# Turning normalised rows by transposing DMA transfers instead of PE products in an attention and GLU kernel

## The chip, the cores and the metric

The kernel runs on one core of one Trainium2 chip. The metric is the device time of one execution in microseconds (us): lower is better. The time given for a kernel is the median of several executions. The kernel before took 911.5 us, the median of three (910.59, 911.5 and 912.72).

The core has a matrix engine (PE; its weight loads are listed apart as PEld), a vector engine (DVE), a scalar engine (ACT), a general engine (POOL), and SP, which here only issues DMA transfers. Each engine runs its own list of instructions in order; one engine waits for another on semaphores.

## The reference

One transformer block on 2048 rows of 640 columns (bf16), with 32 heads of 20 columns each:

```
ln(x) = (x - mean) / sqrt(var + 1e-5)          # over the 640 columns
q, k, v = split(ln(x) @ wqkv)                  # 640 x 1920
p = softmax(q @ k.T * 20**-0.5)                # per head, 2048 x 2048
h = x + concat_heads(p @ v) @ wo
out = h + ((ln(h) @ w_gate) * (ln(h) @ w_up)) @ w_down      # 1728 hidden columns
```

So there are two normalisations. "Layer 1" below is the attention half, "layer 2" the gated half. In each the normalised rows, which lie with 128 rows on the partitions and 640 columns along them, have to be turned, so that the 640 columns lie on the partitions (five blocks of 128 x 128) and can be contracted by PE.

## The kernel before, in words

**Tiling.** The 2048 rows are 16 row tiles of 128, numbered t0 to t15, and four chunks of 512 rows (chunk 0 is t0 to t3). `lnT` holds the turned rows of layer 1 for all 2048 rows; `ln2T` holds those of layer 2 for one block of 512 rows and is used again for each block. The heads are taken four at a time, in eight groups, g0 to g7.

**Score tiles and slots.** The scores are made in PSUM tiles of 128 x 1536 (`emit_S`, L517). There are 683 of them, and the main loop (L1352) goes through them in order: I call one turn of this loop a *slot* and number it like its score tile. In each slot PE makes the scores of the tile (L531), ACT takes their exponential into an SBUF tile `E` (L547), and PE multiplies earlier exponentials with the values (L765, `emit_AV`). There are two score tiles in PSUM and six `E` buffers in SBUF. In some slots DVE takes the last 512 of the 1536 columns over from ACT, with four instructions (L580, L590, L591, L585, `emit_x`); ACT then does 1024 columns only. `x_takes` (L566) decides that by the state of the plan.

**What fills the slots.** All other work is put between the score tiles as jobs: projections of q and k (`job_proj`, L298), of v (`job_V`, L313), and, once the heads of a block of rows are done, the tail of the block: output projection (`job_out`), normalisation of layer 2, gate and up products (`glu_two` and `glu_sum`), down projection (`job_y`). The order is not left to a scheduler. While the program is being built, the kernel keeps a clock for each engine (`at["pe"]`, `at["dve"]`, `at["exp"]`), adds an estimated cost for each step, and puts a job on PE where the estimate leaves room before the next score tile (`run_job`, L499). Vector work that no product waits for at once (statistics, normalisation) stands in a list `aux` and is put in where DVE has time (`spare`, L460). Where PE has too little work to keep its clock up, a pair of products whose results nobody reads is put in (`keep_warm`, L490).

**Layer 1.** `gen_ln` (L861) makes the statistics of a chunk, and `apply1` (L253) normalises a row tile in place in `xs`, in two DVE instructions (L256, L257). For each row tile of chunks 1 to 3 there is a job `T_of` (L882), which calls `job_T` (L276): five PE products against an identity matrix into a PSUM bank (L279) and one DVE copy to `lnT` (L266). The four jobs of chunk n+1 are spread between the key projections of chunk n. Then come the loading of rows for a later chunk and the first key projection of chunk n+1. Chunk 0 is done by itself at the start (`first_T`), with copies on ACT and DVE.

**Layer 2.** The tails are made for (block, first row tile): (0, 0) with four row tiles, then (1, 0), (1, 2), (2, 0), (2, 2) and (3, 0) with two each. That is 14 row tiles. In each, `ln2_pieces` (L1015) makes the normalised row tile on DVE (L239), and `T_pair` inside `job_out` (L1038) turns it by `job_T` into `ln2T`. The last two row tiles are done after the last exponential, in `last_tail` (L1252), which calls `job_T` directly. A path for inputs out of range (`general`) is not run here.

**SP.** All transfers are issued by SP in program order. Beside rows and weights there is a chain for each softmax sum: `sums` out to DRAM (L636) and back (L637), `scr` out (L649) and four `bc` back (L652), each step waiting for the one before to land.

Of the kernel before, what the change touches and what calls it, by code (L numbers as in the profile page):

```python
# [19 lines left out]
P = 128  # L20
# [13 lines left out]
NB = S // QB  # L34
TPB = QB // P
# [15 lines left out]
NEXT = "next slot"  # L51
END = "end"
FREE = "no work for PE"
WAIT = "not yet"
# [8 lines left out]
END_OF_TIME = 10 ** 9  # L63
WARM_LATE, NEXT_DVE = 0, 300
LN_NS = 3300
HOLD_AT, HOLD_NS = 5300, 450
AV_ROUNDS, X_LATE = 2, 0
FULL_IN, FULL_NS, ALL_NS = 2083, 300, 760
# [18 lines left out]
def kernel(  # L87
# [11 lines left out]
    nc = tc.nc  # L99
# [5 lines left out]
    pool = lambda name, bufs=1, **kw: ctx.enter_context(tc.tile_pool(name=name, bufs=bufs, **kw))  # L105
# [37 lines left out]
    lnT = ra.tile([P, KT, S], BF16, name="lnT")  # L143
# [4 lines left out]


    xs = {}  # L150
    now = {"i": 0, "forced": False}
    at = {"pe": 0, "mode": "F", "dve": 0, "dend": 0, "mi": 0, "acc": 0, "slot": [0, 0], "exp": 0, "av": {}}

    def x_tile(ch):
# [86 lines left out]
    lns = {}  # L241
# [19 lines left out]
    def evac(eng, dst, src, ns, last):  # L261
        if eng == "act":
            nc.scalar.copy(dst, src)
        else:
            dve(ns, last)
            nc.vector.tensor_copy(dst, src)  # L266

    end = {"pool": None}

    def bank(dt=F32, w=BANK):  # L270
        if end["pool"] is None:
            return mip.tile([P, w], dt, name="mi", tag="mi")
        ps = end["pool"].tile([P, BANK], F32, name="f", tag="f")
        return ps if dt == F32 else ps[:].bitcast(dt)[:, 0:w]

    def job_T(ln, dst, eng="dve", ps=None, after=None):  # L276
        ps = bank(BF16, D) if ps is None else ps
        for c in range(KT):
            nc.tensor.transpose(ps[:, c * P:(c + 1) * P], ln[:, c * P:(c + 1) * P], ident[:])  # L279
# [98 lines left out]
    def add(key, gen, front=False):  # L378
        (jobs.appendleft if front else jobs.append)((key, gen))
# [22 lines left out]
    def step():  # L402
        if cur["fresh"] and (first() or waiting):
            if cur["gen"] is not None:
                jobs.appendleft((cur["key"], cur["gen"]))
            cur["key"], cur["gen"] = (urgent if first() else waiting).popleft()
        c = advance()
        if c == WAIT:
            waiting.append((cur["key"], cur["gen"]))
            cur["gen"] = None  # L410
            c = advance() if jobs and not any(w[0][1:] == jobs[0][0][1:] for w in waiting) else NEXT
        if c is None:
            return None
        if c == FREE:
            advance()
            return FREE
        if cur["fresh"] and c not in (END, NEXT):
            at["pe"], at["mode"] = max(pe_free("F"), at["mi"] if cur["key"] != ON_ACC else 0), "F"
        cur["fresh"] = c in (END, NEXT)
        if cur["fresh"]:  # L420
            if cur["key"] != ON_ACC:
                at["mi"] = max(at["mi"], at["dend"] + DVE_PE)
        else:
            at["pe"] = pe_free("F") + c
            at["mode"] = "F"
# [14 lines left out]
            return END  # L440

    def ensure(key):
        while key not in done:
            if step() is None:
                raise RuntimeError(f"no job for {key}")

    def step_aux():
        for gen in list(aux):
# [412 lines left out]
    def gen_ln(ch):  # L861
        ts = range(ch * TPB, (ch + 1) * TPB)
        mv = small.tile([P, TPB, 2], F32, name="mv")
        while at["pe"] < x_at.get(ch, END_OF_TIME) and not now["forced"]:
            yield WAIT
        for k in range(TPB):
            yield from bn_pieces(mv, k, xs[ch][:, k, :])
        made = []
        yield from rstd_steps(mv, TPB, made, nc.gpsimd)
        for k, t in enumerate(ts):  # L870
            apply1(t, *made[0], k)
            done.add(("a", t))
            yield 780

    load_x(2)
# [3 lines left out]
    nc.vector.tensor_scalar(q_of(0, 0, 0, QB), pQ[:, 0:QB], shift_row[:, 0:1], None, ALU.add)  # L879
    done.update({("q", 0, 0), ("k", 0, 0)})  # L880

    def T_of(t):  # L882
        ensure_aux(("a", t))
        yield from job_lnT(t)

    aux.append(lead)
    for ch in range(2, NB):
        aux.append(gen_ln(ch))

    for ch in range(NB):  # L890
        nxt = deque(range((ch + 1) * TPB, (ch + 2) * TPB) if ch + 1 < NB else [])

        def one_T():
            if nxt:
                t = nxt.popleft()
                add(("T", t), T_of(t))
        def values(k=0, n=TPB):
            for t in range(ch * TPB + k, ch * TPB + n):
                add(("v", t, 0), job_V(t, 0))
        def keys(g):  # L900
            add(("k", g, ch), job_proj(1, g, ch))
        if ch:
            values(0, 2)
            keys(1)
            values(2)
            for g in range(2, G1):
                keys(g)
                one_T()
        else:
            add(("q", 0, 1), job_proj(0, 1, 0))  # L910
            for _ in range(LEAD):
                step()
            at["pe"] = 0
            keys(1)
            values(0, 3)
            for g in range(2, G1):
                add(("q", 0, g), job_proj(0, g, 0))
                if g == 2:
                    values(3)
                keys(g)  # L920
                one_T()
            one_T()
            one_T()
        while nxt:
            one_T()
        if ch + 1 < NB:
            if ch + 3 < NB:
                do(("x", ch + 3), lambda ch=ch: load_x(ch + 3))
            add(("k", 0, ch + 1), job_proj(1, 0, ch + 1))
# [80 lines left out]
            yield NEXT  # L1010

    ln2 = {"open": 0, "rows": 0}
    COLUMNS_OF = {(1, 0): (0, 0), (1, 2): (0, 0), (2, 0): (1, 0), (2, 2): (1, 2), (3, 0): (2, 0)}

    def ln2_pieces(st, ts, key):  # L1015
        while ln2["open"] >= 2 and not now["forced"]:
            yield WAIT
        ln2["open"] += 1
        mv = small.tile([P, len(ts), 2], F32, name="mv")
        for k, t in enumerate(ts):  # L1020
            yield from bn_pieces(mv, k, st["h"][t][:])
        made = []
        yield from rstd_steps(mv, len(ts), made, nc.gpsimd)
        for k, t in enumerate(ts):
            while ln2["rows"] >= 2 and not now["forced"]:
# [5 lines left out]
            st["l", t] = l_t  # L1031
            done.add(("l2", key, t))
            yield 440

    def job_out(on, st, ts, key):
        pairs = [ts[k:k + 2] for k in range(0, len(ts), 2)]

        def T_pair(pair):  # L1038
            for t in pair:
                while end["pool"] is None and key is not None and (  # L1040
                        ("l2", key, t) not in done or key in COLUMNS_OF and ("glu",) + COLUMNS_OF[key] not in done):
                    yield WAIT
                ensure_aux(("l2", key, t))
                ln2["rows"] -= 1
                yield from job_T(st["l", t], st["ln2T"][:, :, t * P:(t + 1) * P])
                yield NEXT
        done.difference_update({("l2", key, t) for t in ts})
        for k, pair in enumerate(pairs):
            for t in pair:
                yield from out_mm(on, st, t)  # L1050
            if key is not None and k == len(pairs) - 1:
                done.add(("om",) + key)
            aux.append(ln2_pieces(st, pair, key))
            if k:
                yield from T_pair(pairs[k - 1])
        yield from T_pair(pairs[-1])
# [195 lines left out]
    def last_tail():  # L1252
# [98 lines left out]
    i = 0  # L1351
# [136 lines left out]
```

## Time and profile before

| what | value |
|---|---|
| median of three executions | 911.5 us |
| span of the profiled execution | 909.3 us |
| ACT busy | 861.8 us in 719 instructions |
| PE busy | 829.7 us in 8885 products |
| DVE busy | 735.0 us in 1377 instructions |
| transfers | 53.24 MB, 59 GB/s on average |
| granted PE clock | 0.995 of full speed |

The profiled execution was not timed from outside: its own time is known by its span, from the first to the last instruction, and the median of the executions without a profile is 2.2 us longer than that. Where the text works out a time, it does so on the span, and adds 2.2 us at the end.

How the views are read. The page gives busy time by engine, the chain of work that ended last (followed back from the last instruction), and groups of instructions: line, engine, operation, output and input, count, busy time, mean duration, idle time of the engine before them and what ended it. The timeline gives instructions in order of time: start, duration, engine, line, and in brackets the idle time before with its releaser. The windows give busy time by engine and stretch. A few per cent of matmul records are missing from the trace, so counts of matmuls are taken from the program's order of instructions.

### The profile page before, as it was taken

What the parts mean: (1) busy time and instruction counts of PE and PEld (TensorE: products, weight loads), DVE (VectorE), ACT (ScalarE), POOL (GpSimd) and SP (SyncE); (2) the same over time, 40 slices, a digit from 0 to 9 for tenths busy, and PEclk for the clock granted to TensorE, in tenths of its full rate; (3) what the DMA queues carried; (4) which work ended last, traced back from release to release, by engine and by line L of the source; (5) the groups of instructions that cost most, each with busy time, mean ns of one, the idle gap of its engine ahead of it and who ended that gap; (6) DMA issues with size and microseconds to landing.
All of it is one profiled execution on the core that took longest, in us unless ns stands there. A gap on an engine that the chain in (4) does not pass through costs nothing.

```text
span 909.3 us, 21726 instructions
## 1 busy us (share of the span) xinstructions
PE 829.7 (91%) x8885; PEld 371.8 (41%) x8885; DVE 735.0 (81%) x1377; ACT 861.8 (95%) x719; POOL 34.5 (4%) x126
## 2 busy tenths in 40 slices
PE   8888999999999899999989999999999999989997
PEld 5333233222223223344434445444434544435465
DVE  7764359998999999989898989888998989874443
ACT  6999999999999999999999999999999999999941
POOL 3100000000001100001000000010001000010000
PEclk9999999999999999999999999999999999999899
DMA  6000010010042135410203424213360121001310
GB/s 196 30 2 1 1 28 26 14 40 24 2 115 79 45 118 165 112 37 18 62 18 98 109 72 108 66 39 84 93 168 22 50 72 29 3 14 43 80 44 18
DMA packets 90105, 53.24 MB, mean 59 GB/s; under 512 B 24360, under 2 KB 86996, under 8 KB 90000
## 3 DMA queue, kind: packets, MB, share of 16 engines
q1 hardware_dynamic: 90000, 51.80, 21.0%
q8 instruction: 71, 1.16, 0.5%
q14 instruction: 34, 0.28, 0.1%
HBM read 44.49 MB, written 7.28 MB: 57 GB/s over the span
## 4 chain that ended last, share of the span: by engine, by line
ACT 55%; PE 22%; issue 15%; DVE 7%; DMA 1%; SPq 0%; DVEq 0%; ACTq 0%
ACT E L547 55%; PE sc L531 5%; PE mi L1113 3%; PE acc L765 3%; PE mi L1162 3%; PE f L1095 2%; PE f L1162 1%; DVE xv L580 1%; PE mi L1004 1%; DVE u L1118 1%; PE mi L494 1%; DVE xt L591 1%; DVE st L204 0%; DVE xt L590 0%; DVE xe L585 0%
## 5 line engine op out<-in xcount | busy, mean ns | idle before, releaser
L547 ACT ACTIVATE E<-sc 128x1536 bf16<-128x1536 f32 (+1 forms) x683 | 844.3, 1401 | 7.8 <-PE acc L765 3.5
L531 PE MATMUL sc<-qa,kT 32*128 32x256 bf16 (+1 forms) x2176 | 203.0, 318 | 19.0 <-ACT E L547 12.1
L531 PEld LDWEIGHTS <-kT 32*128 32x128 bf16 x3136 | 86.3, 92 | 230.9 <-issue 203.7
L765 PE MATMUL acc<-E,vx 128*32 128x256 bf16 (+1 forms) x2851 | 169.6, 310 | 1.8 <-DVE asb L777 1.0
L580 DVE TENSOR_SCALAR xv<-sc 128x512 f32<-128x512 f32 x179 | 123.5, 690 | 40.1 <-PE sc L531 36.8
L585 DVE SCALAR_TENSOR_TENSOR xe<-xt,xv 128x512 int16<-128x512 f32 x179 | 121.1, 682 | 0.8
L591 DVE SCALAR_TENSOR_TENSOR xt<-xt,xv 128x512 f32<-128x512 f32 x179 | 120.8, 683 | 0.8
L590 DVE SCALAR_TENSOR_TENSOR xt<-xv 128x512 f32<-128x512 uint16 x179 | 119.6, 682 | 0.2
L765 PEld LDWEIGHTS <-vx 128*32 128x32 bf16 x3136 | 65.6, 96 | 68.3 <-issue 65.9
L301 PE MATMUL mi<-lnT,wp 128*128 128x512 bf16 x305 | 85.9, 381 | 8.3 <-DVE qa L308 4.2
L531 PE MATMUL sc<-qb,kT 32*128 32x256 bf16 (+1 forms) x960 | 69.0, 282 | 8.1 <-ACT E L547 7.1
L1162 PE MATMUL mi<-wd,hh 128*128 128x320 bf16 x364 | 64.3, 306 | 1.5 <-DVE xr L1166 1.1
L765 PE MATMUL acc<-xe,vx 128*32 128x256 bf16 (+1 forms) x285 | 56.0, 304 | 0.0
L1162 PEld LDWEIGHTS <-hh 128*128 128x128 bf16 x448 | 38.8, 99 | 30.0 <-issue 17.8
L301 PEld LDWEIGHTS <-wp 128*128 128x128 bf16 x310 | 25.3, 96 | 53.5 <-issue 41.1
L1004 PE MATMUL mi<-wo,on 128*128 128x320 bf16 x224 | 40.9, 301 | 2.6 <-DVE xr L1008 2.0
L1113 PE MATMUL mi<-ln2T,wg 128*128 128x256 bf16 x270 | 39.6, 274 | 3.8 <-DVE u L1118 3.3
L1113 PE MATMUL mi<-ln2T,wu 128*128 128x256 bf16 x270 | 38.7, 274 | 2.1 <-DVE hh L1121 2.0
L308 DVE TENSOR_SCALAR kT<-mi,one_row 128x512 bf16<-128x512 f32 x30 | 22.4, 748 | 21.3 <-PE mi L301 20.9
L494 PE MATMUL mi<-kT,ident 128*128 128x512 bf16 x114 | 34.7, 387 | 2.3 <-DVE ln2T L266 0.8
L1118 DVE CAST u<-mi 128x512 bf16<-128x512 f32 x35 | 24.0, 687 | 12.0 <-PE mi L1113 11.6
L316 PE MATMUL mi<-wv,lnT 128*128 128x320 bf16 x160 | 28.1, 300 | 4.9 <-DVE vx L266 2.9
(143 smaller groups left out, 630.5 us busy)
## 6 DMA issues: line engine op xcount, KB each, us to landing
wu<-in_B_w_up_dram SPq DMA_DIRECT2D x32, 320.0 KB
wg<-in_B_w_gate_dram SPq DMA_DIRECT2D x32, 320.0 KB
bc<-scr SPq DMA_DIRECT2D x60, 64.0 KB
bc<-scr SPq DMA_DIRECT2D x108, 32.0 KB
qsp<-qa SPq DMA_DIRECT2D x8, 384.0 KB
xr<-in_A_x_dram SPq DMA_DIRECT2D x16, 160.0 KB
out_dram<-xr SPq DMA_DIRECT2D x14, 160.0 KB
wd<-in_B_w_down_dram SPq DMA_DIRECT2D x13, 160.0 KB
```

Of the source, the lines that this page charges most:

```text
L301: nc.tensor.matmul(ps[:], lhsT=wslice(m, g, c), rhs=lnT[:, c, ch * QB:(ch + 1) * QB], start=(c == 0), stop=(c == KT - 1))
L494: nc.tensor.matmul(ps[:], lhsT=ident[:], rhs=kT[0][:, 0:BANK], start=True, stop=True)
L531: nc.tensor.matmul(sc[:, o:o + w], lhsT=kT[g][SLOT * j:SLOT * (j + 1), kt * P:(kt + 1) * P], rhs=q_of(g, b, c0, w)[SLOT * j:SLOT * (j + 1) ...
L547: exps = nc.scalar.activation(e[:, 0:n_act], sc[:, 0:n_act], ACT.Exp, bias=EXP_BIAS, scale=SM_SCALE)
L580: took = nc.vector.tensor_scalar(v[:], ps, X_SCALE, X_BASE, ALU.mult, ALU.max)
L585: nc.vector.scalar_tensor_tensor(e[:], t[:], X_R, v[:], ALU.mult, ALU.add)
L590: lambda: nc.vector.scalar_tensor_tensor(t[:], u, X_P, u, ALU.add, ALU.mult),
L591: lambda: nc.vector.scalar_tensor_tensor(t[:], t[:], X_Q, u, ALU.add, ALU.mult),
L765: nc.tensor.matmul(acc["t"][SLOT * j:SLOT * (j + 1), 0:w], lhsT=vx[kt][:, VS * h:VS * h + SLOT], rhs=e, start=(acc["n"][j] == 0), stop=(ac ...
L1004: nc.tensor.matmul(ps[:, 0:HALF], lhsT=on[g][:, t * P:(t + 1) * P], rhs=wo[g][:, cs], start=(g == 0), stop=(g == NG - 1))
L1113: nc.tensor.matmul(ps[:, f2 * n:(f2 + 1) * n], lhsT=st["w", fp][k][:, c, f_cols(fp, f2)], rhs=st["ln2T"][:, c, c0:c0 + n], start=(c == 0), ...
L1162: nc.tensor.matmul(ps[:, 0:HALF], lhsT=st["hh"][f // 2][:, f % 2, t * P:(t + 1) * P], rhs=late["Wd"][f][:, cs], start=(f == 0), stop=(f == ...
```

## The change

In layer 1, chunks 1 to 3, the 12 jobs `T_of` for single row tiles are gone. As soon as a row tile is normalised, an event of the next slot issues one DMA transfer with transpose from `xs` to `lnT` (128 x 640 to 128 x 5 x 128, bf16), on SP. One job per chunk is left, which issues nothing on PE: it waits until PE's planned clock has passed the issue by 2600 ns (`TURN_NS`) for all four row tiles. It stands where the loading of later rows and the first key projection of the next chunk follow. In layer 2, `T_pair` issues such a transfer for each of the 14 row tiles and then waits by the plan in the same way. `last_tail` and chunk 0 are left as they are.

In the order of instructions this takes 26 x 5 products and 26 copies away and adds 26 transfers to SP's list. Since the plan runs on other clocks from slot 10 on, later choices differ too: 17 more `keep_warm` pairs, and 178 blocks of 512 columns taken by DVE in place of 179.

```diff
+TURN_NS = 2600
...
@@ gen_ln
         for k, t in enumerate(ts):
             apply1(t, *made[0], k)
             done.add(("a", t))
+            later(1, lambda t=t: turn(t))
             yield 780
...
-    def T_of(t):
-        ensure_aux(("a", t))
-        yield from job_lnT(t)
+    turned = {}
+
+    def turn(t):
+        if t not in turned:
+            nc.sync.dma_start(lnT[:, :, t * P:(t + 1) * P], lns[t], transpose=True)
+            turned[t] = max(at["pe"], at["dve"]) + TURN_NS
+
+    def T_of(ch):
+        for t in range(ch * TPB, (ch + 1) * TPB):
+            while (t not in turned or at["pe"] < turned[t]) and not now["must"]:
+                yield WAIT
+            if t not in turned:
+                ensure_aux(("a", t))
+                turn(t)
...
         if ch + 1 < NB:
+            add(("T", 0, ch + 1), T_of(ch + 1))
             if ch + 3 < NB:
                 do(("x", ch + 3), lambda ch=ch: load_x(ch + 3))
             add(("k", 0, ch + 1), job_proj(1, 0, ch + 1))
...
@@ T_pair
                 ensure_aux(("l2", key, t))
+                if key is None:
+                    yield from job_T(st["l", t], st["ln2T"][:, :, t * P:(t + 1) * P])
+                    yield NEXT
+                else:
+                    nc.sync.dma_start(st["ln2T"][:, :, t * P:(t + 1) * P], st["l", t][:], transpose=True)
+                    l2_at[key, t] = max(at["pe"], l2_at[key, t]) + TURN_NS
+            for t in pair:
+                while end["pool"] is None and key is not None and at["pe"] < l2_at[key, t]:
+                    yield WAIT
                 ln2["rows"] -= 1
-                yield from job_T(st["l", t], st["ln2T"][:, :, t * P:(t + 1) * P])
-                yield NEXT
```

More of the change, by code (lines that the diff above doesn't have):

```diff
@@ L150 @@
     xs = {}
-    now = {"i": 0, "forced": False}
+    now = {"i": 0, "forced": False, "must": False}
     at = {"pe": 0, "mode": "F", "dve": 0, "dend": 0, "mi": 0, "acc": 0, "slot": [0, 0], "exp": 0, "av": {}}
@@ L442, in ensure @@
     def ensure(key):
+        now["must"] = True
         while key not in done:
@@ L445, in ensure @@
                 raise RuntimeError(f"no job for {key}")
+        now["must"] = False
     def step_aux():
@@ L890 @@
     for ch in range(NB):
[L891 to L896, printed above, removed]
         def values(k=0, n=TPB):
@@ L907 @@
                 keys(g)
-                one_T()
         else:
@@ L920 @@
                 keys(g)
[L921 to L925, printed above, removed]
         if ch + 1 < NB:
+            add(("T", 0, ch + 1), T_of(ch + 1))
             if ch + 3 < NB:
@@ L1012 @@
     ln2 = {"open": 0, "rows": 0}
+    l2_at = {}
     COLUMNS_OF = {(1, 0): (0, 0), (1, 2): (0, 0), (2, 0): (1, 0), (2, 2): (1, 2), (3, 0): (2, 0)}
@@ L1031, in ln2_pieces @@
             st["l", t] = l_t
+            l2_at[key, t] = at["dve"] + 440
             done.add(("l2", key, t))
```

## The prediction, made before the changed kernel ran

> **What bounds the kernel now.** I read the page first, for the engines' shares, the chain that ended last and the costliest group.
>
> ```profile
> span 909.3 us, 21726 instructions
> PE 829.7 (91%) x8885; PEld 371.8 (41%) x8885; DVE 735.0 (81%) x1377; ACT 861.8 (95%) x719; POOL 34.5 (4%) x126
> ACT 55%; PE 22%; issue 15%; DVE 7%; DMA 1%; SPq 0%; DVEq 0%; ACTq 0%
> L547 ACT ACTIVATE E<-sc 128x1536 bf16<-128x1536 f32 (+1 forms) x683 | 844.3, 1401 | 7.8 <-PE acc L765 3.5
> ```
>
> ACT is busy for 95% of the span, 844.3 us of it in the 683 exponentials, and waited only 7.8 us before them. Then I read the windows (each row: stretch, length, busy time of PE, PEld, DVE, ACT and POOL with counts, clock, DMA share, GB/s), to see where the other 5% lies.
>
> ```profile
> 75.00:100.00 25.00, 22.58 (x186) 8.54 (x184) 10.54 (x18) 25.00 (x19) 0.00 (x0) 1.00 0.00 1
> 150.00:200.00 50.00, 46.89 (x336) 14.12 (x334) 47.43 (x80) 50.00 (x42) 0.00 (x0) 1.00 0.08 19
> 880.00:909.00 29.00, 23.67 (x201) 19.21 (x199) 10.21 (x28) 5.21 (x14) 0.00 (x0) 0.97 0.15 42
> ```
>
> In the middle ACT is full; the idle time lies at the start and after the last exponential. Last I read ACT's timeline for its gaps in between.
>
> ```profile
> 15.67 13.75 ACT L547 ACTIVATE E<-sc 128x1536 bf16<-128x1536 f32 x10 [0.66 <-PE sc L531]
> 30.47 13.54 ACT L547 ACTIVATE E<-sc 128x1536 bf16<-128x1536 f32 x10 [1.05 <-PE sc L531]
> 646.87 1.45 ACT L547 ACTIVATE E<-sc 128x1536 bf16<-128x1536 f32 x1 [0.89 <-PE acc L765]
> 863.34 3.76 ACT L547 ACTIVATE E<-sc 128x1536 bf16<-128x1536 f32 x3 [1.65 <-PE sc L531]
> ```
>
> The first exponential, at 15.67, and the three longest gaps are shown; the other gaps that name `acc` (an `E` buffer not yet read by PE) are of 0.2 to 0.6 us, and with the 0.89 make the 3.5 us of the group's row. So three things can change the time: the columns that ACT has to do, a new wait that holds PE until ACT runs dry, and the work after the last exponential. PE and DVE time that is saved elsewhere buys nothing by itself.
>
> **The change part by part.** *What goes.* The copies and the PE products of 26 row tiles:
>
> ```profile
> L266 DVE COPY ln2T<-mi 128x640 bf16<-128x640 bf16 x15 | 7.4, 491 | 3.7 <-PE mi L279 3.7
> L266 DVE COPY lnT<-mi 128x640 bf16<-128x640 bf16 x12 | 5.9, 490 | 7.4 <-PE mi L279 7.4
> 37.45 0.44 PE L279 MATMUL mi<-ident,xs 128*128 128x128 bf16 x5
> 295.89 0.61 PE L494 MATMUL mi<-kT,ident 128*128 128x512 bf16 x2
> ```
>
> DVE loses 26 x 0.49 = 12.7 us and PE 26 x 0.44 = 11.4 us, of which 17 more warming pairs at 0.61 take 10.4 back. DVE could use 12.7 us to take columns from ACT:
>
> ```profile
> L580 DVE TENSOR_SCALAR xv<-sc 128x512 f32<-128x512 f32 x179 | 123.5, 690 | 40.1 <-PE sc L531 36.8
> L585 DVE SCALAR_TENSOR_TENSOR xe<-xt,xv 128x512 int16<-128x512 f32 x179 | 121.1, 682 | 0.8
> L591 DVE SCALAR_TENSOR_TENSOR xt<-xt,xv 128x512 f32<-128x512 f32 x179 | 120.8, 683 | 0.8
> L590 DVE SCALAR_TENSOR_TENSOR xt<-xv 128x512 f32<-128x512 uint16 x179 | 119.6, 682 | 0.2
> ...
> L547 ACT ACTIVATE E<-sc 128x1536 bf16<-128x1536 f32 x503 | 701.6, 1513 | 7.3 <-PE sc L531 3.5 <-PE acc L765 3.1 <-ACT E L547 0.4
> L547 ACT ACTIVATE E<-sc 128x1024 bf16<-128x1024 f32 x180 | 189.4, 1085 | 0.5 <-PE acc L765 0.5
> ```
>
> A block costs DVE 0.690 + 0.682 + 0.683 + 0.682 = 2.74 us and saves ACT 1.513 - 1.085 = 0.43 us. The 12.7 us would pay for 4 blocks, 1.8 us off ACT. But the order of the changed program has 178 blocks, not 180 or more: the plan does not spend what it gains. So ACT does 504 wide and 179 narrow exponentials, **+0.43 us**. The 12 copies to `lnT` fall into the first 100 us anyway, where DVE has time (10.54 of 25 us).
>
> *The 1.05 us gap at 30.47.* In it PE waited for a key copy of chunk 0 on DVE:
>
> ```profile
> 29.99 0.39 PE L531 MATMUL sc<-qa,kT 32*128 32x512 bf16 x1 [0.62 <-DVE kT L308]
> 30.32 0.39 DVE L257 TENSOR_SCALAR xs<-xs,rstd 128x640 bf16<-128x640 bf16 x1
> ...
> 33.98 0.39 DVE L257 TENSOR_SCALAR xs<-xs,rstd 128x640 bf16<-128x640 bf16 x1
> ...
> 41.84 1.24 PE L301 MATMUL mi<-lnT,wp 128*128 128x512 bf16 x5
> ```
>
> Up to slot 10 both programs have the same order, and the gap lies before that. It stays: 0. (The other three rows are used below.)
>
> *The new wait.* A projection or gate product must now wait for a transfer, and PE, which runs in order, would hold the next score tile behind it, and ACT after at most one exponential. What counts is the time L from the end of the normalisation to the landing, against the slots between. No transposing transfer is in the trace. The nearest rows are small transfers of SP, where the next issue waits for the landing, and the queue's total:
>
> ```profile
> 326.36 0.34 SPq L649 DMA_DIRECT2D scr<-ri  x1
> 328.02 1.72 SPq L652 DMA_DIRECT2D bc<-scr  x4
> ...
> 276.47 3.75 SPq L982 DMA_DIRECT2D wd<-in_B_w_down_dram  x8
> ...
> q1 hardware_dynamic: 90000, 51.80, 21.0%
> ```
>
> From `scr` to the first `bc`: 1.66 us for 8 KB, the lower bound of L. For the packets: 21.0% x 16 engines x 909.3 us / 90,000 = 34 ns each (576 B on average). A row tile in pieces of one row of a block (256 B) is 640 packets, 40 per engine, 1.4 us: L = 1.66 + 1.4 = 3.0 us. In pieces of 32 B it is 5,120 packets, 10.9 us, L = 12.5 us: the upper bound. Below nothing the wait cannot go. I take 3.0 us, since 256 B is nearest to the packets that the trace has, and 0.5 us of SP for each issue.
>
> [...]
>
> The distance, from the slots in which the two programs put things: the last normalisation of a set, then its first consumer. Chunk 1: slots 13 and 18; chunk 2: 22 and 31; chunk 3: 31 and 45. Tail (0,0): 224 and 228; (1,0): 334 and 343; (1,2): 373 and 409; (2,0): 483 and 488; (2,2): 548 and 555; (3,0): 644 and 648. A slot is 1.354 us in the row at 30.47 (13.54 / 10) and 851 / 683 = 1.25 us on average (15.7 to 867.1 us). Four places are narrow.
>
> Chunk 1: before, its last row tile was ready at 34.4 (33.98 + 0.39) and its first key product started at 41.8, in slot 19; one slot earlier is 40.5, so 6.1 us are there, 3.1 to spare. Tail (3,0): 5.0 us for the second transfer of a pair, 0.5 + 3.0 = 3.5. Tail (2,0): 6.2 us for the same. Tail (0,0): 5.0 us; ahead of its last pair SP has an `scr`, four `bc` (1.66 + 1.72 us by the rows above) and a weight load from slots 222 and 223, and one more weight load (3.75 / 8 = 0.5 each): 4.4 us of issue in 2.5 us, 1.9 us behind when slot 224 begins, and some 1.4 when its normalisation ends. Landing 1.4 + 0.5 + 3.0 = 4.9 us after, against 5.0. With an uncertainty of half a slot that is a wait of 0 to 0.9 us; I take **0.4**. Everything else SP has behind the transfers (weights, sums) is due slots later; if a transfer held SP for 2 us in place of 0.5, the second of a pair would come 1.5 us later, which only (0,0) would feel, by 1.4 us. SP itself waits for DVE at each transfer, with the sums chain queued behind, but the transfer is put in a slot after its normalisation, so that wait is short.
>
> *The end.* `last_tail` is unchanged, but the leftover down products (L1162) fall otherwise.
>
> ```profile
> 875.57 1.04 DVE ln L1291 x2
> 876.61 0.41 DVE xr L1166
> 877.02 0.04 issue
> 877.06 0.44 PE mi L279 x5
> 877.50 0.28 PE acc L279 x5
> 877.78 2.72 PE f L1162 x20
> ```
>
> In this chain the 0.41 us is the drain of a half row of down products that stood in the bank that the turn needs. In the changed order that half is done ahead of the tail, so the 0.41 goes; but 24 products, not 20, stand after the turn: 4 x 2.72 / 20 = 0.54. **+0.13 us.** What is late next is the same product line.
>
> *Sum.* 0.43 + 0.4 + 0.13 = +1.0 us: span 910.3, and with 2.2 us (911.5 - 909.3) **912.5 us**, +0.1%. A measurement of this kernel can tell about 0.2% (1.8 us) from no change.
>
> **The rivals.**
>
> *A slower kernel: the five blocks of a transfer pay a round trip each.* L = 5 x 1.66 = 8.3 us. Place: PE, before the first product of a set. Prices: chunk 1 8.3 - 6.1 = 2.2; (0,0) 1.4 + 0.5 + 8.3 - 5.0 = 5.2; (2,0) 0.5 + 8.3 - 6.2 = 2.6; (3,0) 0.5 + 8.3 - 5.0 = 3.8: 13.8 us, less some 0.5 of cover at each place: 12. 909.3 + 12 + 0.6 + 2.2 = 924. It decides from L = 4.5 us on, where (0,0) alone gives 1.4 us and (3,0) begins. For it: nothing in the trace bounds it away. Against: no transfer in the trace pays more than one round trip. With L between 4.5 and 8.3 the time lies between 913 and 924.
>
> *Far slower: 32 B pieces.* 10.9 us of all 16 engines for each row tile: the four of chunk 1, from 31 us on, end near 31 + 1.7 + 43.6 = 76, 36 us late; the pairs of four tails some 15 us each: about 1,005 us. Against: the packets would be a sixteenth of the trace's mean.
>
> *Faster: the freed DVE time closes ACT's waits for `E`.* Those 3.5 us come where AV products stand late behind a drain of DVE. If all went: 909.3 + 0.43 + 0.13 - 3.5 + 2.2 = 908.6. For: DVE is full there (47.43 of 50 us). Against: few of the gaps lie near a turn, and a new order makes new ones.
>
> **How the numbers follow.** Forecast (L up to 4.5 us): 0.65, and 909.5 to 915. Five round trips, or part of them: 0.20. 32 B pieces: 0.04. Faster: 0.11. The range is 909.5 to 919: it leaves out the faster case, the far case and the upper half of the first rival. Slower by over 0.2%: 0.24 of the two slow rivals and 0.13 of the forecast's 0.65; within: the other 0.52; faster: 0.11.
>
> **What would show it.** Right: DVE busy near 720 us (735 - 12.7 - 2.7); ACT's exponentials at 844.7 us; the last exponential ends within 2 us of 867 us; the transfers land about 3 us after issue; PE waits for a transfer of `ln2T` once, near slot 228. Wrong: PE waits for `lnT` near 40 us or at three or more tails; SP held by a transfer for over 1.5 us; ACT's wait before exponentials over 11 us, or under 5. If L is over 4.5 us, the wait term fails; if ACT's waits move by more than 2 us with no transfer in them, the new order did it and not the transfers.

## The result, and the profile after

The kernel after takes 917.23 us (median of five executions, 914.82 to 917.68), against 911.5 us before: a ratio of 1.0055, with a 95% interval of 1.0037 to 1.0073. It is slower by 5 to 6 us. The profiled execution took 917.35 us, with a span of 915.5 us; before, the span was 909.3 us. So I explain 6.2 us of span.

First the page of the kernel after: the span, the engines, the chain that ended last, the group of exponentials (busy us and mean ns, then idle us before them and its main releaser) and the queue of SP.

```profile
span 915.5 us, 21572 instructions
PE 832.1 (91%) x8787; PEld 365.7 (40%) x8787; DVE 721.8 (79%) x1347; ACT 863.5 (94%) x719; POOL 33.7 (4%) x126
q1 hardware_dynamic: 107472, 56.06, 23.7%
ACT 57%; PE 16%; issue 14%; DVE 10%; DMA 2%; SPq 0%; DVEq 0%; ACTq 0%
L550 ACT ACTIVATE E<-sc 128x1536 bf16<-128x1536 f32 (+1 forms) x683 | 846.0, 1400 | 12.4 <-PE sc L534 10.6
```

DVE lost 13.2 us of work, of 15.4 reckoned (12.7 of copies and one block of columns), and it bought nothing. ACT still bounds the kernel: its exponentials are busy for 1.7 us longer than before and wait 4.6 us longer. That is the whole loss, since the first one starts 0.17 us earlier and what follows the last is 42.2 us in both. The transfers' share of the chain rises from 1 to 2%.

Next ACT's timeline (start, duration, group, and in brackets the idle time before it), cut to the gap near 30 us that the prediction left where it is, and to the places where new waits came:

```profile
30.31 12.20 ACT L550 ACTIVATE E<-sc 128x1536 bf16<-128x1536 f32 x9 [1.05 <-PE sc L534]
43.55 1.45 ACT L550 ACTIVATE E<-sc 128x1536 bf16<-128x1536 f32 x1 [1.04 <-PE sc L534]
46.09 1.45 ACT L550 ACTIVATE E<-sc 128x1536 bf16<-128x1536 f32 x1 [1.09 <-PE sc L534]
48.50 72.68 ACT L550 ACTIVATE E<-sc 128x1536 bf16<-128x1536 f32 x54 [0.96 <-PE sc L534]
...
310.98 1.02 ACT L550 ACTIVATE E<-sc 128x1024 bf16<-128x1024 f32 x1 [1.85 <-PE sc L534]
312.73 4.13 ACT L550 ACTIVATE E<-sc 128x1536 bf16<-128x1536 f32 x3 [0.72 <-PE sc L534]
...
581.30 1.02 ACT L550 ACTIVATE E<-sc 128x1024 bf16<-128x1024 f32 x1 [1.66 <-PE sc L534]
582.83 1.45 ACT L550 ACTIVATE E<-sc 128x1536 bf16<-128x1536 f32 x1 [0.51 <-PE sc L534]
584.79 35.38 ACT L550 ACTIVATE E<-sc 128x1536 bf16<-128x1536 f32 x29 [0.51 <-PE sc L534]
```

The 1.05 us near 30 stayed. There are three new places: 3.1 us near 45 in this execution (other executions of the same order lost less there, as the experiments show), 2.7 us near 311 (with a last 0.16 at 317), 2.7 us near 581; 8.5 us together. In return the waits on `acc` fell from 3.5 to 1.2 us and the 1.65 us at 863 is gone: 8.5 - 2.3 - 1.65 = 4.6. Now the windows at these places; the column to look at is the third from the right, PE's granted clock.

```profile
35.00:40.00 5.00, 3.02 (x28) 0.65 (x24) 1.68 (x4) 5.00 (x5) 1.96 (x6) 0.80 0.48 88
40.00:45.00 5.00, 4.49 (x20) 1.44 (x16) 3.15 (x8) 3.96 (x3) 0.00 (x0) 0.50 0.29 108
...
310.00:315.00 5.00, 5.00 (x22) 1.23 (x22) 2.58 (x4) 3.29 (x3) 0.00 (x0) 0.66 0.12 37
...
580.00:585.00 5.00, 5.00 (x60) 2.19 (x57) 3.70 (x7) 2.68 (x3) 0.00 (x0) 0.66 0.30 62
```

At all three the clock fell, to 0.50, 0.66 and 0.66: PE is busy for 4.5 to 5 us of 5, but with products that take longer (three score products 0.61 us at 40.05, where the clock is 0.50, and 0.39 at 48.70, where it is 1.00). So each place has a first cause that left PE without work, and a slow spell behind it.

**Near 311 us, tail (0, 0).** The rows of DVE's normalisation, of SP's queue and of PE:

```profile
302.48 0.80 DVE L240 TENSOR_SCALAR ln<-xr,m,rstd 128x640 bf16<-128x640 bf16 x2
...
303.05 1.73 SPq L655 DMA_DIRECT2D bc<-scr  x4
304.83 0.90 SPq L986 DMA_DIRECT2D wd<-in_B_w_down_dram  x2
305.83 2.53 SPq L1054 DMA_TRANSPOSE ln2T<-ln  x2
...
309.97 0.59 PE L1108 MATMUL mi<-ln2T,wu 128*128 128x512 bf16 x2 [2.11 <-issue]
```

The rows are normalised at 303.28. SP issues their two transfers only at 305.83, behind four `bc` and two weight loads, and each holds it for 1.26 us; the product that needs them starts at 309.97, after 2.11 us in which PE stood.

**Near 45 us, chunk 1.** Here no product waits for a transfer. SP, then DVE, then PE:

```profile
30.58 5.96 SPq L890 DMA_TRANSPOSE lnT<-xs  x4
37.91 0.37 SPq L163 DMA_DIRECT2D xs<-in_A_x_dram  x1
...
42.15 0.49 DVE L210 BATCH_NORM_STATS2 st<-xs 128x6 f32<-128x320 bf16 x1 [1.29 <-DMA xs<-in_A_x_dram]
...
43.20 0.70 DVE L309 TENSOR_SCALAR kT<-mi,one_row 128x512 bf16<-128x512 f32 x1
...
40.59 2.31 PE L302 MATMUL mi<-lnT,wp 128*128 128x512 bf16 x5
43.95 1.49 PE L317 MATMUL mi<-wv,lnT 128*128 128x320 bf16 x5 [0.51 <-DVE kT L309]
```

The rows of chunk 3 go into the buffer from which the transfers of chunk 1 read, so their load stands behind these (37.91). DVE comes to their statistics 1.29 us before they are there, and the key copy that PE's value products wait for stands behind. The load is not late against the kernel before, where it was issued at 41.29 and DVE came to these statistics only at 47.03. It is late against the new plan, which put the statistics 4.9 us earlier. And five key products take 2.31 us, against 1.24 in the kernel before, with the clock at 0.50 here and at 1.00 there: in 35 to 40 PE had 3.02 us of work in 5 us, in the kernel before 4.21.

**Near 581 us.** No transposing transfer is near. SP, DVE, PE:

```profile
572.41 0.51 SPq L639 DMA_DIRECT2D sums<-asb  x1
575.76 0.35 SPq L640 DMA_DIRECT2D sums_all<-sums  x1
...
578.22 0.20 DVE L650 RECIPROCAL ri<-sums_all 128x8 f32<-128x8 f32 x1 [1.72 <-DMA sums_all<-sums]
...
579.43 1.25 PE L1175 MATMUL mi<-wd,hh 128*128 128x320 bf16 x8 [1.85 <-DVE xr L1179]
```

The sums of a pass go out right behind two weight loads, and DVE can read them only 5.8 us after that issue; DVE stands at their reciprocal for 1.72 us, and PE behind DVE for 1.85.

My theory after this: (T) the transposing transfers cost the time near 311, by SP's queue; (R) the late rows and thin slots cost that near 45; (S) the late sums cost that near 581, and that is an effect of the new order. The rival to all three: the new order as such costs the time, whatever transposes.

### The profile page after: what moved, and what is told of

Its sections match the earlier page's. It is cut to its first block, busy times and chain, and to the rows that moved or that the text cites. A ratio compares the mean times of both kernels' runs of the same rounds, so it can differ in the third digit from the quotient of the medians.

```text
span 915.5 us, 21572 instructions
## 1 busy us (share of the span) xinstructions
PE 832.1 (91%) x8787; PEld 365.7 (40%) x8787; DVE 721.8 (79%) x1347; ACT 863.5 (94%) x719; POOL 33.7 (4%) x126
## 3 DMA queue, kind: packets, MB, share of 16 engines
q1 hardware_dynamic: 107472, 56.06, 23.7%
## 4 chain that ended last, share of the span: by engine, by line
ACT 57%; PE 16%; issue 14%; DVE 10%; DMA 2%; SPq 0%; DVEq 0%; ACTq 0%
ACT E L550 57%; PE sc L534 3%; PE mi L1126 3%; PE acc L768 2%; PE f L1108 2%; DVE xv L583 1%; PE f L1175 1%; DVE xt L593 1%; DVE xt L594 1%; PE mi L1108 1%; PE mi L302 1%; DVE xe L588 1%; PE mi L317 1%; PE mi L1175 1%; DMA ln2T<-ln 1%
## 5 line engine op out<-in xcount | busy, mean ns | idle before, releaser
L550 ACT ACTIVATE E<-sc 128x1536 bf16<-128x1536 f32 (+1 forms) x683 | 846.0, 1400 | 12.4 <-PE sc L534 10.6
L1175 PE MATMUL mi<-wd,hh 128*128 128x320 bf16 x350 | 62.2, 304 | 3.9 <-DVE xr L1179 3.7
L768 PE MATMUL acc<-xe,vx 128*32 128x256 bf16 (+1 forms) x282 | 53.7, 306 | 0.0
L497 PE MATMUL mi<-kT,ident 128*128 128x512 bf16 x148 | 44.7, 384 | 2.7 <-DVE xr L1012 0.6
L267 DVE CAST vx<-mi 128x320 bf16<-128x320 f32 x32 | 15.7, 492 | 23.3 <-PE mi L317 23.1
```

The costliest lines, as they stand in the source:

```text
L497: nc.tensor.matmul(ps[:], lhsT=ident[:], rhs=kT[0][:, 0:BANK], start=True, stop=True)
L550: exps = nc.scalar.activation(e[:, 0:n_act], sc[:, 0:n_act], ACT.Exp, bias=EXP_BIAS, scale=SM_SCALE)
L768: nc.tensor.matmul(acc["t"][SLOT * j:SLOT * (j + 1), 0:w], lhsT=vx[kt][:, VS * h:VS * h + SLOT], rhs=e, start=(acc["n"][j] == 0), stop=(ac ...
L1175: nc.tensor.matmul(ps[:, 0:HALF], lhsT=st["hh"][f // 2][:, f % 2, t * P:(t + 1) * P], rhs=late["Wd"][f][:, cs], start=(f == 0), stop=(f == ...
```

## The experiments

All ratios are to the kernel before, run on the same chip beside the experiment. "Narrow" is the number of exponentials of 1024 columns (each saves 0.43 us); waits and exponentials are those of the group's row on each page.

| kernel | narrow | exponentials, us | waits, us | median, us | ratio (95%) |
|---|---|---|---|---|---|
| before | 180 | 844.3 | 7.8 | 911.5 | 1 |
| after | 179 | 846.0 | 12.4 | 917.23 | 1.0055 (1.0037 to 1.0073) |
| plain | 179 | 845.3 | 6.7 | 912.8 | 1.0016 (1.0001 to 1.0030) |
| layer1_alone | 182 | 844.0 | 7.7 | 909.1 | 0.9971 (0.9952 to 0.9990) |
| layer2_alone | 176 | 846.3 | 7.6 | 913.93 | 1.0033 (1.0011 to 1.0054) |
| warm_early | 177 | 846.3 | 10.4 | 918.54 | 1.0089 (1.0060 to 1.0119) |
| rows_late | 179 | 845.9 | 10.7 | 916.43 | 1.0065 (1.0039 to 1.0090) |
| l1_rows | 182 | 844.0 | 7.1 | 908.49 | 0.9965 (0.9949 to 0.9980) |
| l1_rows_warm | 178 | 845.4 | 6.7 | 910.93 | 1.0008 (0.9993 to 1.0023) |
| rows_5000 | 182 | 843.8 | 9.6 | 909.43 | 0.9979 (0.9963 to 0.9995) |
| twice_00 | 179 | 846.0 | 23.7 | 929.09 | 1.0181 (1.0149 to 1.0213) |
| rows_late_sums_8000 | 180 | 845.0 | 15.0 | 917.5 | 1.0062 (1.0042 to 1.0083) |
| rows_5000_sums_8000 | 179 | 845.0 | 10.0 | 915.75 | 1.0039 (1.0026 to 1.0053) |

### Plain transfers in the same order

```
-nc.sync.dma_start(lnT[...], lns[t], transpose=True)
+nc.sync.dma_start(lnT[...], lns[t].rearrange("p (c k) -> p c k", k=P))     # both layers
```

The rows are not turned in this one; everything else, the order too, is that of the kernel after.

> The changed kernel with plain transfers of the same 26 row tiles in place of transposing ones: the rows are moved and not turned, so what follows computes with unturned rows. The order of every engine is that of the changed kernel. It tells what belongs to the transposing (SP held 1.24 us, landing about 3 us) from what belongs to the order. G: the first place stays (3.1 us), the place at 580 us stays (2.7 us, a reciprocal that waits for its sums), and the first tail at 310 us shrinks from 2.7 us to under 1, since SP is held 0.5 us and the landing is quicker; span 912.5 to 914.5. W: all three places shrink, span near 909 to 911. If transposing transfers slow the others in flight too, 580 us changes as well.

How long SP is held by one transfer (shortest, median, longest, in ns), first in `plain`, both layers:

```profile
L890 SPq DMA_DIRECT2D lnT<-xs x12: 593/594/794, 31.2 to 61.1; - x12
L1054 SPq DMA_DIRECT2D ln2T<-ln x14: 610/645/668, 294.6 to 814.3; - x14
```

and then in the kernel after:

```profile
L890 SPq DMA_TRANSPOSE lnT<-xs x12: 1200/1228/2004, 30.6 to 64.8; - x12
L1054 SPq DMA_TRANSPOSE ln2T<-ln x14: 1205/1244/1762, 296.7 to 821.0; - x14
```

A transposing transfer held SP for about twice as long as a plain one of the same size: medians of 1.23 and 1.24 us against 0.59 and 0.65. In `plain`'s timeline the wait near 311 shrinks to one of 0.91 us at 308.02, and the clock there is 1.00. The wait near 580 stays, but is 1.59 us in place of 2.7: DVE stands for the same late sums, and the clock did not fall (1.00 from 570 to 585). The waits near 45 shrink to 0.52 us, where I had expected 3.1. The time is 912.8 us, 0.16% above before. So the transposing itself costs about 1.0055 - 1.0016 = 0.4% (0.2 to 0.6 by the two intervals), most of the loss, and the rival that the order alone costs it falls. How much of it each place has isn't settled by these two profiled executions, since the place near 45 differs between executions of one order (below). The place near 580 belongs to the order.

### One layer at a time

`layer1_alone` keeps the transfers of layer 1 and gives `T_pair` back its PE products; `layer2_alone` is the reverse.

```
 ensure_aux(("l2", key, t))                                   # layer1_alone
-nc.sync.dma_start(st["ln2T"][...], st["l", t][:], transpose=True)
+ln2["rows"] -= 1
+yield from job_T(st["l", t], st["ln2T"][...])
...                                                           # the loop that waits for l2_at is gone too
```

> The change in layer 1 only; layer 2 turns by PE as before. Theory (G): the loss of 8.5 us of exponential waits in the changed kernel sits at three places where PE stood idle for about 2 us and the granted clock fell to 0.5 to 0.66. The first, 40 to 50 us, has no product that waits for a landing: the planned 2600 ns leave slots 14 to 17 without full-width work. So this kernel must show the first place as it was: ACT waits of about 3.1 us between 40 and 50 us and a clock near 0.5 in 40 to 45 us, and no such place at 310 us. The order has 182 narrow exponentials against 180 before, 0.9 us less of ACT. Span 909.3 + 3.1 - 0.9, 911 to 913; ratio to before 1.000 to 1.005. Rival (W, transfers that land late hold PE everywhere): a wait for a landing of lnT of over 1 us in the trace, at chunks 2 and 3 also; ratio 1.005 or more.

> The change in layer 2 only; layer 1 turns by PE as before. G: no wait between 40 and 50 us, clock 1.0 there. At the first tail the turns stand again four slots before the gate product (227 and 231), behind the sums chain on SP: PE idle of 1 to 2 us and exponential waits of 1.5 to 3 us near 310 us. The order has 176 narrow exponentials, 1.7 us more of ACT. Span 909.3 + 1.7 + 2.5, 912 to 915; ratio 1.003 to 1.007. Rival (the new order as such costs, not the transfers): no idle PE of over 1 us at the first tail, and the time lost at places with no transfer.

With layer 1 alone the kernel is faster than before, which I had not expected: the place near 45 costs 1.18 us, not 3.1, the other two are not there, 182 exponentials are narrow, and some former gaps are gone. A new place near 460 costs 1.8 us. With layer 2 alone it is slower. In its windows the place near 311 has the same slow spell (2.2 us of ACT's waits lie there):

```profile
310.00:315.00 5.00, 4.45 (x28) 0.96 (x29) 4.89 (x9) 3.37 (x3) 0.00 (x0) 0.66 0.08 20
```

and its view of waits (who waited for whom: us in total, times, longest) shows a second way in which a transfer holds things up, DVE's waits before the normalisation of the second pair:

```profile
DVE ln L240 <- DMA ln2T<-ln: 2.7, 2, 1.8
```

It writes into the buffers that the first pair's transfers have not yet read. But the loss of `layer2_alone` is not one of waits in sum (7.6 us against 7.8): its exponentials are busy 2.0 us longer, 4 x 0.43 = 1.7 of it from four fewer narrow ones. So the loss is with layer 2, and it isn't one of the waits near 311 alone.

### Warming earlier, and rows later

For the place near 45, `warm_early` lets warming pairs in from slot 12 on; `rows_late` has the plan count 4 us more until the rows of chunk 3 are there; `l1_rows` is `rows_late` with layer 1 alone, and `l1_rows_warm` has all three edits.

```
-if i > WARM and not ran ...                                  # warm_early
+if i > 11 and not ran ...
-x_at[ch] = at["pe"] + ROWS_NS if ch > 1 else 0               # rows_late
+x_at[ch] = at["pe"] + ROWS_NS + 4000 * (ch == 3) if ch > 1 else 0
```

> The changed kernel, with the warming pair allowed from slot 12 on (before: from slot 59 on); the plan puts pairs into slots 14, 15 and 16. G: the clock stays at 1.0 between 35 and 50 us and the 3.1 us of ACT waits there fall under 0.5; the first tail (turn in slot 224, product in slot 228) still costs its 2.7 us. The order has 177 narrow exponentials, 0.4 us more. Span 911 to 914, ratio to before 1.002 to 1.005, 2 to 4 us under the changed kernel. W: the first place keeps its 3 us, since the rows land no sooner; span 915 to 917.

> The changed kernel, in which the plan looks for the last chunk's rows 4 us later; the order from slot 40 on is the same as in the changed kernel. Theory R: at 40 to 50 us it is neither the landing of turned rows nor the clock alone, but DVE: it waits 1.3 to 1.9 us for the rows of chunk 3, whose load had to wait until the transfers had read the same buffer (issue at 37.9 us), and the drain of chunk 1's key product stands behind. With the statistics later that wait is 0, the drain comes at about 41.5 and not 43.2, and the ACT waits in 40 to 50 us fall from 3.1 us to under 1. Span 912.3 to 914; ratio to before 1.001 to 1.005. Rival (the clock alone, from thin slots 14 to 17): the waits stay over 2 us, since those slots are as thin; span 915 to 916.5.

> Layer 1 by transfers, layer 2 by PE, and the rows of the last chunk looked for 4 us later: the order of the layer 1 run except in slots 14 to 36. R: its 1.2 us of waits at 43 and 45 us go (under 0.4), the span falls from 907.9 to 906.5 to 907.3, and the ratio to before is 0.994 to 0.998. Rival (clock): the waits stay, 907.5 to 908.5.

> As the one before, with warming pairs allowed from slot 12 on (slots 14, 15, 16). If the clock in 40 to 45 us had a price of its own, this is where it shows: the clock stays 1.0 there, and the waits fall by what was left. The order has only 178 narrow exponentials against 182, 1.7 us more. R: span 908 to 909.5, slower than the one before. Clock: 907 or less.

ACT's waits near 45: after 3.1 us; with warming 1.34 us (the clock is 1.00 in all windows from 35 to 50, but DVE still stands 1.9 us for the rows); with the rows late 0.79 us (no wait for rows, the clock at 0.76 in 40 to 45); with the rows late, warming and layer 1 alone none, clock 1.00.

These figures need a comparison that I had not set out to make. Up to slot 224 `layer1_alone` and `twice_00` (below) have the order of the kernel after, with no remedy. Yet `layer1_alone` waits 1.18 us here and `twice_00` 0.89, against 3.1, although DVE stands for the rows in them too (1.66 and 1.42 us):

```profile
43.86 1.45 ACT L550 ACTIVATE E<-sc 128x1536 bf16<-128x1536 f32 x1 [0.65 <-PE sc L534]
...
42.49 0.49 DVE L210 BATCH_NORM_STATS2 st<-xs 128x6 f32<-128x320 bf16 x1 [1.42 <-DMA xs<-in_A_x_dram]
...
40.00:45.00 5.00, 4.23 (x20) 1.36 (x16) 3.14 (x8) 4.35 (x4) 0.00 (x0) 0.67 0.34 121
```

(These are from `twice_00`; the second wait of ACT is 0.24 us.) In the kernel after the clock was at 0.50 in 40 to 45 and at 0.68 in 45 to 50; here it was at 0.67 in 40 to 45, and three score products take 0.39 us again from 43.36 on, after 0.61 at 40.58. So some 2 of the 3.1 us belong to a longer slow spell in that one execution, and the fall from 3.1 to 1.34 or 0.79 us can't be credited to an edit. The five kernels with the rows late and no early warming range from 0.57 to 1.61 us. What does show the two causes is `l1_rows_warm`, which has no wait and up to slot 224 differs from the others by these edits alone: against `warm_early` it takes away the late rows alone, worth 1.34 us, and against those five it adds the warming alone, worth 0.6 to 1.6. That is one profiled execution of each.

In `warm_early` and `rows_late` the total did not follow: in the former two fewer narrow exponentials cost 0.86 us; in the latter the span fell by 2.3 us (913.2, of the shortest of its four executions) but the median by 0.8 only, with a ratio that can't be told from that of the kernel after. `l1_rows` is the best kernel of all, 0.35% faster than before. `l1_rows_warm` loses that again, though its waits are fewest: 4 fewer narrow exponentials cost 1.7 us.

### A longer time for the transfers in the plan

```
-l2_at[key, t] = max(at["pe"], l2_at[key, t]) + TURN_NS       # 2600
+l2_at[key, t] = max(at["pe"], l2_at[key, t]) + 5000          # on top of rows_late
```

> As the one before, and the plan gives the transfers of layer 2 5000 ns in place of 2600. The first tail then has seven slots between the last turn (226) and the gate product (233). If the wait at the first tail is the transfer behind SP's queue, it goes there (2.7 us to under 0.5), and at no other tail does PE wait. The order has 182 narrow exponentials against 179, 1.3 us less. Span 915.5 - 2.5 - 2.5 - 1.3, 908.5 to 910.5; ratio 0.998 to 1.002. If the first tail's wait has another cause (a new order as such), it moves to another place of the same size, and the span is 911.5 to 913.

The place near 311 is gone (ACT runs from 278.76 to 345.95 without a wait; the clock is 1.00 from 305 to 315), and the kernel is 0.2% faster than before (0.9979, 0.9963 to 0.9995), with all 26 transfers in it. Its profiled execution was the longest of its ten (912.75 us), and has 4.1 us of waits left near 576, where DVE stands for late sums and the clock falls to 0.53. So T's remedy worked at its place. The time fell by 7.0 us against `rows_late`: 2.7 of it is this place and 1.3 the three more narrow exponentials, an effect of the new order. How much of the rest is the order's I can't say.

### The transfers of (0, 0) issued twice

```
+for _ in range(1 + (key == (0, 0))):
     nc.sync.dma_start(st["ln2T"][...], st["l", t][:], transpose=True)
```

> The kernel after, with each of the four transfers of the place (0, 0) issued twice; everything else, the order too, as it was. Theory SP: the 2.1 us for which PE stands still near 310 us are set by SP, which a transposing transfer holds for about 1.24 us, so the second copies of the pair put the last landing off by 1.2 to 2.5 us, and both PE's idle time there and ACT's waits (2.73 us) grow by that, to 4 to 5 us; the time rises by 2 us or so. Rival: PE waits there for the normalising on VectorE or for a weight, and the copies change nothing (waits of 2.5 to 3 us).

SP, PE and ACT in this kernel's timeline:

```profile
311.23 8.05 SPq L1055 DMA_TRANSPOSE ln2T<-ln  x4
...
320.92 1.01 PE L1109 MATMUL mi<-ln2T,wu 128*128 128x512 bf16 x2 [14.64 <-DMA ln2T<-ln]
...
322.57 1.02 ACT L550 ACTIVATE E<-sc 128x1024 bf16<-128x1024 f32 x1 [15.02 <-PE sc L534]
```

PE waits at the same product, now 14.64 us instead of 2.11, and the time rises by 11.9 us (929.09 against 917.23). The sign is that of the SP theory and the size far over my 2 us. I had left out that a second copy waits on SP for the first to land, so that a pair with its copies holds SP for 8.05 us, where the pair alone takes 2.53, and that (0, 0) has two such pairs, one behind the other: SP is done with them at 319.28, in the kernel after at 308.36, 10.9 us earlier. The rival (PE waits for DVE or a weight) falls: the 10.9 us by which SP was put off came out at PE (12.5 us more) and at ACT (13.2 us more in the first gap). PE has 1.6 us more than SP because this execution was that much ahead here: its last product before the gap starts at 305.67, in the kernel after at 307.24. The row gives an estimate of the landing too: 8.05 us taken as four holds of 1.206 us (the median here) and two waits for a landing leave 1.6 us for each wait, so a transfer landed 1.6 us after SP was free again, 2.8 us after its issue; 320.92 - 319.28 = 1.64 us says the same.

### Sums expected later

```
-WO_NS, SUMS_NS, ROOT_NS, ROWS_NS = 1500, 6000, 5000, 5000
+WO_NS, SUMS_NS, ROOT_NS, ROWS_NS = 1500, 8000, 5000, 5000    # on top of rows_late, and of rows_5000
```

> The kernel after, with the rows of chunk 3 normalised 4 us later in the plan, and with the sums of a pass expected back after 8 instead of 6 us, so that VectorE takes their reciprocal later. Theory S: the waits at 577 to 585 us (2.7 to 2.9 us) come from VectorE standing before a reciprocal whose sums have not landed; with 2 us more the longest wait for sums falls under 0.5 us and these waits of ACT under 0.8 us; 180 instead of 179 narrow exponentials cost 0.4 us; time 2 us under the kernel after, about 914 to 915. Rival: the place is short of work for PE whatever the sums do, and 2 us or more of waits stay there.

> The same, and the plan also counts 5.0 instead of 2.6 us from the issue of a transfer in the second layer to its columns. By S and by the theory that the plan's 2.6 us was too short, all three places go: ACT waits 1 us or less at each, 179 narrow exponentials (1.3 us saved on 182), 906.5 to 908.5 us, under the kernel before and as good as the one with the change in layer 1 alone. By the rival the waits move elsewhere, and it stays at 909 to 913.

S was right for its place: in both kernels the waits from 577 to 585 us are gone; among DVE's waits none for sums is left in the first, and one of 1.3 us, elsewhere, in the second. The time wasn't: 917.5 and 915.75 us, not 914 and 907. In the first, transfers now meet other work on SP. Near 311 DVE stands for buffers which the transfers, issued behind four `bc`, have not yet read, and near 631 PE stands for the transfers themselves, issued at 627.29 behind four `bc` and the two transfers of sums:

```profile
308.26 0.45 DVE L240 TENSOR_SCALAR ln<-xr,m,rstd 128x640 bf16<-128x640 bf16 x1 [3.54 <-DMA ln2T<-ln]
...
312.56 1.45 ACT L550 ACTIVATE E<-sc 128x1536 bf16<-128x1536 f32 x1 [2.58 <-PE sc L534]
...
627.29 2.56 SPq L1054 DMA_TRANSPOSE ln2T<-ln  x2
...
631.24 1.16 PE L1126 MATMUL mi<-ln2T,wu 128*128 128x256 bf16 x9 [1.81 <-DMA ln2T<-ln]
632.96 2.37 ACT L550 ACTIVATE E<-sc 128x1024 bf16<-128x1024 f32 x2 [1.85 <-PE sc L534]
```

In the second, no transfer is late, but 4.9 us of waits for `acc` came elsewhere, and a spell of low clock near 410 (0.55 in 410 to 415). So one repaired place doesn't make the kernel faster: the plan chooses anew behind it, and what it chooses is worth as much as the repair.

## Why the prediction was right, and where its sizes were off

The forecast was 912.5 us, the range 909.5 to 919; the time is 917.23, in the range and in the upper part of it. The cases called slower had 0.37, and slower it is, but the likeliest outcome, within 0.2% of before, had 0.52.

That the time lies in the range is in good part luck. For a landing of up to 4.5 us the prediction gave 909.5 to 915; it added 915 to 919 for landings that cost several round trips. The landing took 2.9 us, so it is the forecast's own case that holds, and the range of that case is missed by 2 us, through terms that the sum had at nothing. Two of the signs written down say the same: ACT's wait before exponentials is 12.4 us, over the 11 that were to mean wrong, and the last exponential ends at 873.3, not within 2 us of 867. Step by step:

**ACT bounds the kernel, and saved work on DVE and PE buys nothing: right.** DVE fell to 721.8 us (reckoned: 720), and the loss is all in ACT's exponentials and their waits.

**The columns, +0.43 us: right, but not the whole.** 504 wide and 179 narrow exponentials, as counted. Their busy time rose by 1.7 us, not 0.43. One behind a gap shows 1.45 us (43.55), one in a row of them 12.20 / 9 = 1.36 (30.31), so by these rows each new gap costs about 0.1 us more than itself. ACT's timelines have 16 gaps before exponentials after and 12 before, so this makes up some 0.4 of the other 1.3; the cause of the remaining 0.9 stays open.

**L = 3.0 us: right.** Near 311 the second transfer was issued at 305.83 + 1.26 = 307.09 and its columns were used at 309.97, 2.9 us later; the copies in `twice_00` give 2.8. The first rival (five round trips, 8.3 us) and the 32 B pieces did not come: 17,472 more packets for 26 transfers are 672 each, near the 640 of the forecast. What the forecast had too small is the time that a transfer holds SP: 1.24 us (the median in layer 2) against the 0.5 us taken, and against 0.65 for a plain one in `plain`.

**The wait at (0, 0), 0.4 us: the right place and cause, mis-sized.** It was the term that I took as 1.4 (SP behind) + 0.5 (one issue) + 3.0 against 5.0. (With half a slot, 0.63 us, either way that sum gives 0 to 0.5 us, not the 0 to 0.9 written there.) Measured: 2.55 us behind, 1.26 for the first transfer, 2.9 for the second, 6.7 us from the end of the normalisation at 303.28, against 4.6 until PE was free at 307.85: 2.1 us, which is the row's 2.11. Of the miss, 1.15 us is SP's queue ahead of the pair, 0.76 the longer hold and 0.4 the shorter distance. The prediction had named the case of a transfer that holds SP longer (2 us) and priced it at 1.4 us more, at (0, 0) only; that was the right direction. What it did not have is the step behind: the clock. Behind PE's idle 2.11 us it was at 0.66 in 310 to 315, after 1.00 in 305 to 310, and ACT lost 2.7 us in place of 2.1.

**Chunk 1, cost 0: wrong by 0.9 to 3.1 us, as the execution falls.** The products did not wait for the transfers, as forecast. But the step counted only the readers of `lnT`. It left out who writes into `xs` next (the load of chunk 3, which now waits 1.2 us for transfers, and whose rows the new plan expects too early) and what is left on PE in slots from which the turns were taken out: 3.02 us of work in 35 to 40, with the clock at 0.50 behind it, where `warm_early` has 4.43 us and the clock at 1.00. `rows_late` took away DVE's wait for the rows, `warm_early` the slow clock, and only both together the waits of ACT.

**Where a stall goes: the order.** The prediction gave the faster case (the waits for `acc` close) 0.11. It came in part, 2.3 us of 3.5, and with the 1.65 us at 863 about 4 us were gained, but the new order made 2.7 us of waits near 581 for late sums. The sign written down for that ("if ACT's waits move by more than 2 us with no transfer in them, the new order did it") fits what `plain` shows there: a wait of 1.59 us for the same sums with no transposing in it. The rest of the 2.7 came with the clock (0.66 in 580 to 585, in `plain` 1.00).

**The end, +0.13 us:** 42.2 us in both.

So the parts of the sum of +1.0 were real, but they are the smaller part of the true +6.2. In the profiled execution there come to them 3.1 us near 45, 2.3 more near 311, 2.7 near 581 and 1.3 of longer exponentials, less the 4 us of former gaps that I had not taken.

## What to carry to other kernels

The work that went here from DVE and PE to the DMA queue took its waits to that queue: price a transfer by how long it holds the issuing engine (1.24 us here), by what stands ahead of it there (2.55 us at (0, 0)), and by who writes into its source next (DVE stood 1.29 us for the rows of chunk 3), not only by when its reader needs it. Where an engine that feeds the bound runs with little slack, work taken from it is not always a gain: with 2.9 to 3.0 us of PE's work in 35 to 40, the clock in 40 to 45 was 0.50 to 0.77 in eight kernels that have the transfers of layer 1 and no warming there (after, `plain`, `layer1_alone`, `rows_late`, `l1_rows`, `rows_5000`, `twice_00`, `rows_late_sums_8000`); with 4.1 to 4.4 us of work it was 1.00 in the two with warming. And where a plan orders the work, compare versions with the same order, or repair one wait and expect the plan to make another. Last, look at one place in several runs that share the order up to it before an edit is credited with what it lost there.

## What the hardware showed that I had not expected

A transposing SBUF-to-SBUF transfer of 128 x 640 bf16 held SP's queue for a median of 1.23 us in layer 1 and 1.24 in layer 2 (1.20 to 2.00 in all), a plain one of the same size for 0.59 and 0.65 (0.59 to 0.79), though it moves the same bytes (56.06 MB on the queue in both kernels).

PE's clock fell after short gaps. In the trace of the kernel after it is at 0.50 from 37.99 to 48.23, from 311.06 to 314.47 and from 580.71 to 584.12, and at 1.00 just before and behind each. The two later spells last 3.41 us each, the first one 10.24 us, three times as long, and all six times are whole multiples of 10.24 / 3 = 3.413 us apart. PE's gaps ahead of the later two were 2.11 and 1.85 us. Near the last of these places in `plain` PE's gap was 1.96 us and the clock stayed at 1.00, so no gap of about 2 us settles it by its length. Where the gap falls may, which is my guess: in the kernel after each of the two gaps lies inside one step of this length that ends where the slow spell begins, and in it PE is busy for 1.31 us (307.64 to 311.06) and 1.55 us (577.30 to 580.71). Little work in a stretch was not always followed by a slow spell: in `warm_early` PE is busy for 2.45 us in 40 to 45, and the clock is 1.00 there and in 45 to 50; in the kernel after PE is busy for 2.54 us in 305 to 310, and the clock is 0.66 in 310 to 315. So a limit doesn't come out of these runs.
